# Small q, go, out and dq transfers moved from the POOL queue to the sync queue of an attention backward kernel, with the stores queued early

## The chip, the cores and the metric

The kernel runs on one core of a Trainium2 chip. The metric is device time in microseconds (us) of that core. A ratio is the mean time of one kernel's fast runs over the mean time of the other's fast runs of the same rounds, with a 95% interval; so it is not quite the ratio of the medians that are quoted. "SyncE" (SP in the profile) is the engine that issues the large transfers; "the sync queue" is its hardware DMA queue (q1), "the POOL queue" is the software DMA queue (q0) that POOL issues.

## The reference

Grouped attention with its gradients: 32 batches, 32 query heads, 4 key/value heads, 4 query rows, 2048 keys, head size 128, bfloat16.

```python
B, Hq, Hkv, Sq, Sk, D = 32, 32, 4, 4, 2048, 128
def _fwd_reference(q, k, v):                 # k, v repeated 8 times over the heads
    scores = jnp.einsum("bhqd,bhkd->bhqk", q, k) * D ** -0.5
    p = _softmax(scores, axis=-1)
    return jnp.einsum("bhqk,bhkd->bhqd", p, v)
def reference(q, k, v, grad_out):
    _out, _vjp = jax.vjp(_fwd_reference, q, k, v)
    return (_out, *_vjp(grad_out))           # out, dq, dk, dv
```

Each batch reads 2 MB of K and 2 MB of V and writes 2 MB of dK and 2 MB of dV, in transfers of 1 MB. Beside them are four small transfers of 32 KB a batch: q and go (grad_out) in, out and dq out. In all 274 MB move, of which the small ones are 4.2 MB.

## The kernel before

The program is a list of units (one matmul group, one eviction, one transfer), each with a planned time `PLACE` plus a correction `SHIFT` for the first three and last four batches. The planned times are used only to sort: every engine and every DMA queue then runs its units in that order, waiting where a result is missing.

```python
DMA, SMALL = "SP", "POOL"
PERIOD = 21.3
PLACE = dict(LQ=[-47.936], LK=[...], LV=[3.599, 0.95], ..., Oe=[18.672], Os=[94.455],
    DQe=[52.911], DQs=[136.569], ..., DVs=[39.32, 39.758], DKs=[48.837, 48.854], ...)
# [cut: SHIFT of batches 0, 1, 2 and of the last four, -4 to -1]
u.at = b * PERIOD + PLACE[name][i] + (SHIFT[special][name][i] if special in SHIFT else 0.0)
return sorted(order, key=lambda u: u.at), bank_of

sm_pool = pool("small", 4)                    # q, go, o, dq: four buffers each
if name == "LQ":                              # loads q and go of a batch
    t["q"] = sm_pool.tile([P, D], BF16, name="q_sb")
    nc.gpsimd.dma_start(out=t["q"][:], in_=q_r[b])
    t["go"] = sm_pool.tile([P, D], BF16, name="go_sb")
    nc.gpsimd.dma_start(out=t["go"][:], in_=go_r[b])
elif name in ("LK", "LV"):                    # 1 MB each
    nc.sync.dma_start(out=whole[:, h], in_=src[b, g][:, h])
elif name in ("Os", "DQs"):                   # stores of out and dq; Oe, DQe evict them
    nc.gpsimd.dma_start(out=(o_r if name == "Os" else dq_r)[b], in_=...)
elif name in ("DVs", "DKs"):                  # 1 MB each; the last batch uses halves, DVh and DKh
    nc.sync.dma_start(out=(dv_r if name == "DVs" else dk_r)[b, g], in_=...)
```

## Time and profile before

692.51 us, median of three runs (691.18 to 692.68). The page of the profiled run; the third line is the busy share of the 16 DMA engines in 40 slices, in tenths, and the last is the chain that ended last, by line.

```profile
span 688.6 us, 28403 instructions
...
PE 620.1 (90%) x12352; PEld 467.1 (68%) x12352; DVE 558.3 (81%) x776; ACT 604.4 (88%) x921; POOL 208.8 (30%) x426
...
DMA  9999999999999999999999999999999999999967
GB/s 347 403 413 387 415 414 409 415 415 416 415 416 416 414 416 412 397 407 413 408 409 405 410 412 414 399 398 412 405 412 405 406 401 397 408 403 386 391 260 263
...
q1 hardware_dynamic: 70784, 268.45, 97.6%
q0 software_dynamic: 4096, 4.20, 1.8%
...
DMA v_sb<-in_v_dram 52%; PE psum L372 10%; PE psum L477 6%; ACT dk_sb L483 4%; ACT dv_sb L483 4%; PE psum L431 3%; DMA out_dram<-dv_sb 2%; ACT e_sb L399 2%; PE psum L442 2%; ACT vt_sb L337 2%; POOL dop_sb_103 L411 1%; PE psum L383 1%; DVE kt_sb L390 1%; ACT kt_sb L337 1%; DMA go_sb<-in_grad_out_dram 1%
```

The DMA engines are full in all but the last two slices. Total time is therefore the work of DMA, plus whatever time DMA is made to stand idle, plus the end of the last batch.

The timeline of SyncE (start, us taken, line, what, count) shows it held by queue room, 2.3 to 2.6 us for a 1 MB issue:

```profile
437.64 2.41 SPq L358 DMA_DIRECT2D k_sb<-in_k_dram  x1
440.17 4.67 SPq L492 DMA_DIRECT2D out_dram<-dv_sb  x2
```

The last two slices by windows (window, its us, busy us of PE, PEld, DVE, ACT, POOL, granted clock, DMA share, GB/s), and the whole of SyncE's end:

```profile
654.20:671.40 17.20, 14.27 (x310) 10.23 (x310) 14.47 (x22) 13.97 (x20) 6.80 (x15) 1.00 0.67 260
671.40:688.60 17.20, 8.04 (x200) 5.22 (x196) 8.83 (x9) 6.72 (x10) 1.42 (x3) 0.88 0.73 263
```

```profile
652.89 1.00 SPq L492 DMA_DIRECT2D out_dram<-dv_sb  x2
665.05 0.88 SPq L492 DMA_DIRECT2D out_dram<-dk_sb  x2
669.70 4.89 SPq L488 DMA_DIRECT2D out_dram<-dv_sb  x4
676.83 3.70 SPq L488 DMA_DIRECT2D out_dram<-dk_sb  x4
```

### The profile page before, as it was taken

The numbers are of one execution on the slowest core, as the hardware profiler recorded it, in microseconds if no ns is written. First come the engines' busy times: TensorE is split into PE (matmuls) and PEld (weight loads), VectorE is DVE, ScalarE is ACT, GpSimd is POOL, SyncE is SP. The second block draws the span as 40 slices with busy tenths as digits, with TensorE's granted clock in tenths as the row PEclk, the third lists the DMA queues.
The fourth block names the chain that finished last, engine by engine and source line by source line (L and its number), as shares of the span: only waits on it lengthen the run. The fifth ranks groups of instructions, "written<-read, shape, count | busy, mean of one in ns | idle before, by whom it ended". The sixth has DMA issues, their size and how long they took to land.

```text
span 688.6 us, 28403 instructions
## 1 busy us (share of the span) xinstructions
PE 620.1 (90%) x12352; PEld 467.1 (68%) x12352; DVE 558.3 (81%) x776; ACT 604.4 (88%) x921; POOL 208.8 (30%) x426
## 2 busy tenths in 40 slices
PE   5899999999999999999999899998889998989984
PEld 4677677777677777766667666676666766766753
DVE  3788888888889888888788878787787887888885
ACT  2889999999999999998899888899888998888883
POOL 2423321333322233331233321333212333113330
PEclk9999999999999999999999999999999999999998
DMA  9999999999999999999999999999999999999967
GB/s 347 403 413 387 415 414 409 415 415 416 415 416 416 414 416 412 397 407 413 408 409 405 410 412 414 399 398 412 405 412 405 406 401 397 408 403 386 391 260 263
DMA packets 75005, 274.47 MB, mean 399 GB/s; under 512 B 6272, under 2 KB 6272, under 8 KB 74880
## 3 DMA queue, kind: packets, MB, share of 16 engines
q1 hardware_dynamic: 70784, 268.45, 97.6%
q0 software_dynamic: 4096, 4.20, 1.8%
q8 instruction: 96, 1.57, 0.8%
q14 instruction: 29, 0.24, 0.1%
HBM read 136.31 MB, written 136.31 MB: 396 GB/s over the span
## 4 chain that ended last, share of the span: by engine, by line
DMA 55%; PE 22%; ACT 13%; issue 5%; POOL 3%; DVE 2%; SPq 0%; POOLq 0%; DVEq 0%; ACTq 0%
DMA v_sb<-in_v_dram 52%; PE psum L372 10%; PE psum L477 6%; ACT dk_sb L483 4%; ACT dv_sb L483 4%; PE psum L431 3%; DMA out_dram<-dv_sb 2%; ACT e_sb L399 2%; PE psum L442 2%; ACT vt_sb L337 2%; POOL dop_sb_103 L411 1%; PE psum L383 1%; DVE kt_sb L390 1%; ACT kt_sb L337 1%; DMA go_sb<-in_grad_out_dram 1%
## 5 line engine op out<-in xcount | busy, mean ns | idle before, releaser
L483 ACT CAST dk_sb<-psum 128x1024 bf16<-128x1024 f32 x159 | 157.6, 1013 | 25.9 <-PE psum L477 24.5
L483 ACT CAST dv_sb<-psum 128x1024 bf16<-128x1024 f32 x155 | 151.7, 1022 | 13.2 <-PE psum L477 12.4
L372 PE MATMUL psum<-ident,v_sb 128*128 128x128 bf16 x2048 | 147.4, 220 | 16.8 <-DMA v_sb<-in_v_dram 15.3
L372 PEld LDWEIGHTS <-v_sb 128*128 128x128 bf16 x2048 | 117.9, 98 | 56.9 <-issue 32.8
L372 PE MATMUL psum<-ident,k_sb 128*128 128x128 bf16 x2048 | 142.4, 221 | 10.2 <-ACT dk_sb L483 10.2
L372 PEld LDWEIGHTS <-k_sb 128*128 128x128 bf16 x2048 | 121.4, 99 | 27.1 <-issue 24.3
L483 DVE CAST dv_sb<-psum 128x1024 bf16<-128x1024 f32 x101 | 122.8, 1220 | 10.8 <-PE psum L477 10.6
L483 DVE CAST dk_sb<-psum 128x1024 bf16<-128x1024 f32 x97 | 115.9, 1219 | 8.5 <-ACT kt_sb L337 4.5
L337 ACT COPY kt_sb<-psum 128x512 f32<-128x512 f32 x190 | 110.3, 595 | 6.6 <-PE psum L372 5.1
L411 POOL TENSOR_SCALAR dop_sb_103<-go_sb,rinv 32x128 bf16<-32x128 bf16 x64 | 38.5, 602 | 225.4 <-DVE rinv L404 97.3
L411 POOL TENSOR_SCALAR dop_sb_102<-go_sb,rinv 32x128 bf16<-32x128 bf16 x64 | 38.5, 602 | 212.5 <-DVE rinv L404 141.1
L463 DVE SCALAR_TENSOR_TENSOR ds_sb<-psum,delta,e_sb 128x1024 bf16<-128x1024 f32 x64 | 81.9, 1279 | 15.1 <-ACT vt_sb L337 13.5
L337 ACT COPY vt_sb<-psum 128x512 f32<-128x512 f32 x131 | 75.5, 599 | 17.6 <-PE psum L372 16.6
L340 DVE COPY vt_sb<-psum 128x1024 bf16<-128x1024 bf16 x125 | 82.9, 681 | 2.9 <-PE psum L372 2.6
L477 PEld LDWEIGHTS <-e_sb 64*128 64x128 bf16 x1024 | 50.0, 93 | 36.3 <-issue 19.6
L399 ACT ACTIVATE e_sb<-psum,m 128x1024 bf16<-128x1024 f32 x64 | 71.1, 1122 | 2.4 <-DVE kt_sb L390 2.2
L340 DVE COPY kt_sb<-psum 128x1024 bf16<-128x1024 bf16 x66 | 44.9, 685 | 18.8 <-PE psum L372 18.8
L477 PEld LDWEIGHTS <-ds_sb 64*128 64x128 bf16 x1024 | 43.3, 94 | 23.8 <-issue 8.8
L477 PE MATMUL psum<-dop_sb_103,e_sb 64*128 64x256 bf16 x512 | 45.2, 270 | 4.1 <-POOL dop_sb_103 L411 1.6
L477 PE MATMUL psum<-dop_sb_102,e_sb 64*128 64x256 bf16 x512 | 44.9, 270 | 3.2 <-ACT dv_sb L483 0.7
L390 DVE TENSOR_SCALAR_CACHE_REDUCE kt_sb<-psum 128x1024 bf16<-128x1024 f32 x32 | 39.2, 1225 | 9.6 <-issue 7.7
L390 DVE TENSOR_SCALAR_CACHE_REDUCE kt_sb<-psum,m 128x1024 bf16<-128x1024 f32 x32 | 41.1, 1284 | 6.5 <-DVE kt_sb L390 3.9
(83 smaller groups left out, 764.5 us busy)
## 6 DMA issues: line engine op xcount, KB each, us to landing
k_sb<-in_k_dram SPq DMA_DIRECT2D x62, 1024.0 KB, 18.7
v_sb<-in_v_dram SPq DMA_DIRECT2D x62, 1024.0 KB, 19.6
out_dram<-dv_sb SPq DMA_DIRECT2D x62, 1024.0 KB, 19.0
out_dram<-dk_sb SPq DMA_DIRECT2D x62, 1024.0 KB, 18.8
k_sb<-in_k_dram SPq DMA_DIRECT2D x4, 512.0 KB, 5.4
v_sb<-in_v_dram SPq DMA_DIRECT2D x4, 512.0 KB, 9.4
out_dram<-dv_sb SPq DMA_DIRECT2D x4, 512.0 KB, 7.9
out_dram<-dk_sb SPq DMA_DIRECT2D x4, 512.0 KB, 6.7
```

Source lines behind the costliest of these rows:

```text
L337: nc.scalar.copy(out=out.rearrange("p c d -> p (c d)").bitcast(FP32), in_=in_.rearrange("p c d -> p (c d)").bitcast(FP32))
L340: nc.vector.tensor_copy(out=out, in_=in_)
L372: nc.tensor.transpose(out=ps[:, j, :], in_=t[x, h][:, 8 * i + j, :], identity=ident[:])
L383: nc.tensor.matmul(t[name, i][r, QW * w:QW * w + QW], lhsT=t["qdt"][:, side, r], rhs=t[x, h, i][:, CPQ * w:CPQ * w + CPQ, :], start=True, ...
L390: nc.vector.tensor_scalar(out=spent, in0=t["S", i][:], scalar1=-scale, scalar2=t["m"][:] if i else None, op0=ALU.mult, op1=ALU.min, accum_ ...
L399: nc.scalar.activation(out=t["e"][:, 2 * QW * i:2 * QW * i + 2 * QW], in_=t["S", i][:], func=ACT.Exp, bias=t["m"][:], scale=scale, accum_o ...
L411: nc.gpsimd.tensor_scalar(out=t["dop"][r, h % 2, :], in0=t["go"][r, :], scalar1=t["rinv"][r, :], scalar2=None, op0=ALU.mult)
L431: nc.tensor.transpose(out=ps[:, j, :], in_=src[:, P * c:P * c + P], identity=ident[:])
L442: nc.tensor.matmul(t[name][r, 0:D], lhsT=t[xt, c // 8][:, c % 8, r], rhs=t[x, h][:, c, :], start=(c == 0), stop=(c == C - 1), tile_positio ...
L463: nc.vector.scalar_tensor_tensor(out=t["ds"][:, w], in0=t["DP", i][:], scalar=t["dl"][:], in1=t["e"][:, w], op0=ALU.subtract, op1=ALU.mult)
L477: nc.tensor.matmul(accs[g][:, 2 * P * j:2 * P * j + 2 * P], lhsT=t[lhs][r, P * c:P * c + P], rhs=t[rhs][r, :, :].rearrange("p h d -> p (h ...
L483: copy(out=t[name[:2], "out", g][:, :, CPQ * i:CPQ * i + CPQ, :], in_=t[name[:2], i][g][:].rearrange("p (c h d) -> p h c d", h=2, d=D))
```

## The change

The intent: one hardware queue for all transfers, no software descriptors, and the o and dq buffers freed early. On POOL the stores stood four batches after their results, in pairs. Now they stand 6.3 us (out) and 6.1 us (dq) of the plan after the eviction, and in the first three and last four batches they take the same SHIFT as the eviction. The place of the q and go loads (LQ) is not changed, only their queue.

```diff
-    O=[...], Oe=[18.672], Os=[94.455], DQ=[...], DQe=[52.911],
-    DQs=[136.569], ...
+    O=[...], Oe=[18.672], Os=[25.0], DQ=[...], DQe=[52.911],
+    DQs=[59.0], ...
# [cut: in each of the seven SHIFT tables Os becomes Oe's value and DQs becomes DQe's, e.g.]
-        Oe=[158.875], Os=[319.648], DQe=[601.801], DQs=[743.423],
+        Oe=[158.875], Os=[158.875], DQe=[601.801], DQs=[601.801],
@@ LQ
-            nc.gpsimd.dma_start(out=t["q"][:], in_=q_r[b])
+            nc.sync.dma_start(out=t["q"][:], in_=q_r[b])
-            nc.gpsimd.dma_start(out=t["go"][:], in_=go_r[b])
+            nc.sync.dma_start(out=t["go"][:], in_=go_r[b])
@@ Os, DQs
-            nc.gpsimd.dma_start(out=(o_r if name == "Os" else dq_r)[b], in_=...)
+            nc.sync.dma_start(out=(o_r if name == "Os" else dq_r)[b], in_=...)
```

More of the change, by code (lines that the diff above doesn't have):

```diff
@@ L30 @@
     qp=[18.579], rs=[18.682], ET=[13.658, 17.08], ETe=[14.252, 17.097], DT=[33.736, 36.072], DTe=[35.413, 37.066],
-    O=[17.693, 18.002, 18.156, 18.29], Oe=[18.672], Os=[94.455], DQ=[49.509, 49.546, 51.434, 51.658], DQe=[52.911],
-    DQs=[136.569], DL=[19.54], qfree=[23.411], ofree=[103.245], rfree=[77.997], DP=[19.952, 20.297, 32.139, 32.573],
+    O=[17.693, 18.002, 18.156, 18.29], Oe=[18.672], Os=[25.0], DQ=[49.509, 49.546, 51.434, 51.658], DQe=[52.911],
+    DQs=[59.0], DL=[19.54], qfree=[23.411], ofree=[103.245], rfree=[77.997], DP=[19.952, 20.297, 32.139, 32.573],
     DS=[20.684, 33.191], DV=[17.102, 19.055, 20.709, 23.293], DVe=[18.269, 19.578, 20.009, 20.012, 22.48, 21.535,
@@ L47 @@
         qp=[-26.573], rs=[12.305], ET=[-63.892, -40.448], ETe=[-47.865, -38.526], DT=[-4.086, -0.412], DTe=[-3.298,
-        6.139], O=[-39.845, -33.444, -32.183, -28.165], Oe=[-27.877], Os=[-59.712], DQ=[1.765, 2.888, 1.329, 1.269],
-        DQe=[1.892], DQs=[-81.021], DL=[-24.403], qfree=[-3.591], ofree=[-33.901], rfree=[9.398], DP=[-14.103,
+        6.139], O=[-39.845, -33.444, -32.183, -28.165], Oe=[-27.877], Os=[-27.877], DQ=[1.765, 2.888, 1.329, 1.269],
+        DQe=[1.892], DQs=[1.892], DL=[-24.403], qfree=[-3.591], ofree=[-33.901], rfree=[9.398], DP=[-14.103,
         -13.278, -0.13, 0.179], DS=[-3.43, 2.07], DV=[-22.144, -22.96, -21.745, -14.349], DVe=[-21.142, -24.454,
@@ L60 @@
         0.721], L=[7.117], dop=[8.675], qp=[10.349], rs=[25.4], ET=[1.855, 2.426], ETe=[1.513, 3.358], DT=[13.036,
-        7.483], DTe=[12.538, 6.893], O=[3.459, 3.832, 3.884, 5.102], Oe=[4.915], Os=[-60.332], DQ=[0.889, 1.045,
-        -0.411, 0.94], DQe=[0.233], DQs=[-25.356], DL=[5.409], qfree=[12.194], ofree=[-66.5], rfree=[13.969],
+        7.483], DTe=[12.538, 6.893], O=[3.459, 3.832, 3.884, 5.102], Oe=[4.915], Os=[4.915], DQ=[0.889, 1.045,
+        -0.411, 0.94], DQe=[0.233], DQs=[0.233], DL=[5.409], qfree=[12.194], ofree=[-66.5], rfree=[13.969],
         DP=[6.763, 7.072, 3.675, 3.981], DS=[7.015, 3.749], DV=[6.331, 5.5, 3.952, 3.37], DVe=[5.694, 4.344, 4.713,
@@ L73 @@
         qp=[5.002], rs=[10.293], ET=[1.766, 0.607], ETe=[1.259, 1.305], DT=[0.213, -2.004], DTe=[-0.525, -2.044],
-        O=[1.246, 1.5, 1.545, 1.726], Oe=[1.403], Os=[-52.917], DQ=[1.425, 1.546, 0.484, 0.395], DQe=[-0.47],
-        DQs=[-55.959], DL=[0.669], qfree=[3.492], ofree=[-33.606], rfree=[5.069], DP=[1.794, 1.829, 0.034, -0.258],
+        O=[1.246, 1.5, 1.545, 1.726], Oe=[1.403], Os=[1.403], DQ=[1.425, 1.546, 0.484, 0.395], DQe=[-0.47],
+        DQs=[-0.47], DL=[0.669], qfree=[3.492], ofree=[-33.606], rfree=[5.069], DP=[1.794, 1.829, 0.034, -0.258],
         DS=[2.187, -0.275], DV=[3.733, 2.494, 1.983, 0.34], DVe=[2.697, 1.941, 1.905, 2.434, 1.012, 1.581, 0.049,
@@ L85 @@
         qp=[7.309], rs=[42.149], ET=[2.195, -1.278], ETe=[1.919, -1.171], DT=[4.743, 3.278], DTe=[5.609, 3.25],
-        O=[-1.322, -1.479, 0.528, 1.287], Oe=[1.058], Os=[87.413], DQ=[8.174, 8.908, 7.1, 7.978], DQe=[8.064],
-        DQs=[153.09], DL=[1.413], qfree=[433.476], ofree=[379.582], rfree=[188.9], DP=[2.141, 2.215, 0.855, 0.51],
+        O=[-1.322, -1.479, 0.528, 1.287], Oe=[1.058], Os=[1.058], DQ=[8.174, 8.908, 7.1, 7.978], DQe=[8.064],
+        DQs=[8.064], DL=[1.413], qfree=[433.476], ofree=[379.582], rfree=[188.9], DP=[2.141, 2.215, 0.855, 0.51],
         DS=[2.76, 0.829], DV=[2.494, 0.835, 0.895, 0.758], DVe=[1.61, 0.109, 1.229, 0.024, -0.073, 2.137, -1.76,
@@ L97 @@
         dop=[6.256], qp=[8.124], rs=[52.601], ET=[1.369, 4.066], ETe=[2.632, 4.831], DT=[11.561, 14.267],
-        DTe=[13.249, 14.741], O=[4.22, 3.956, 3.979, 4.659], Oe=[5.161], Os=[124.411], DQ=[53.76, 58.627, 71.647,
-        76.742], DQe=[81.838], DQs=[178.343], DL=[4.74], qfree=[223.784], ofree=[169.959], rfree=[350.347],
+        DTe=[13.249, 14.741], O=[4.22, 3.956, 3.979, 4.659], Oe=[5.161], Os=[5.161], DQ=[53.76, 58.627, 71.647,
+        76.742], DQe=[81.838], DQs=[81.838], DL=[4.74], qfree=[223.784], ofree=[169.959], rfree=[350.347],
         DP=[4.904, 5.645, 9.011, 8.772], DS=[5.688, 11.455], DV=[4.558, 4.643, 5.415, 6.214], DVe=[4.631, 4.282,
@@ L110 @@
         qp=[19.591], rs=[195.2], ET=[16.601, 13.645], ETe=[17.156, 15.506], DT=[91.107, 112.344], DTe=[91.851,
-        123.716], O=[14.871, 15.992, 19.77, 20.459], Oe=[24.605], Os=[65.93], DQ=[226.498, 229.962, 296.861,
-        321.979], DQe=[324.799], DQs=[716.368], DL=[24.893], qfree=[188.487], ofree=[315.264], rfree=[471.673],
+        123.716], O=[14.871, 15.992, 19.77, 20.459], Oe=[24.605], Os=[24.605], DQ=[226.498, 229.962, 296.861,
+        321.979], DQe=[324.799], DQs=[324.799], DL=[24.893], qfree=[188.487], ofree=[315.264], rfree=[471.673],
         DP=[25.295, 26.106, 46.944, 48.701], DS=[28.132, 55.939], DV=[14.792, 16.553, 22.109, 26.604], DVe=[14.274,
@@ L124 @@
         128.051], DT=[266.776, 395.941], DTe=[293.717, 431.921], O=[134.296, 138.938, 140.503, 143.271],
-        Oe=[158.875], Os=[319.648], DQ=[364.485, 371.073, 501.046, 588.268], DQe=[601.801], DQs=[743.423],
+        Oe=[158.875], Os=[158.875], DQ=[364.485, 371.073, 501.046, 588.268], DQe=[601.801], DQs=[601.801],
         DL=[177.07], qfree=[296.09], ofree=[481.606], rfree=[573.081], DP=[203.332, 207.071, 280.92, 280.696],
@@ L452, in emit @@
         elif name in ("Os", "DQs"):
-            nc.gpsimd.dma_start(out=(o_r if name == "Os" else dq_r)[b], in_=t["o" if name == "Os" else "dq"][:])
+            nc.sync.dma_start(out=(o_r if name == "Os" else dq_r)[b], in_=t["o" if name == "Os" else "dq"][:])
         elif name == "DL":
```

## The prediction

> **What bounds the kernel now.** The DMA engines. The page's DMA row is 9 tenths in 38 of 40 slices; the hardware queue takes 97.6% of 16 engines' span, the software queue 1.8% (4.2 of 274 MB). PE is busy 90%, ACT 88%. The chain of waits is V loads back to back from 276 to 616 us, 21.05 us a batch; before that compute sets the pace (20.3 us a batch) while DMA is already full (415 GB/s; later about 405). The timeline of SyncE shows the later stretch limited by queue room: a 1 MB issue takes 2.3 to 2.6 us, against 0.4 us when there is room, and lands 19 us later. The last 34 us (DMA 0.67 and 0.73) are compute and store latency.
>
> **What the change moves.** 128 transfers of 32 KB (4 a batch) leave POOL (0.54 to 0.61 us each, 73 us off an engine that is 30% busy: worth nothing) for SyncE's in-order queue, about 0.4 us an issue. The Trainium skill, "DMA: Bandwidth & Descriptors", section "Issuing engines are not separate DMA queues", says all issuers end on the same 16 engines, so I expect no bandwidth from it; slow 4 KB packets in this trace do not cluster at the software packets either.
>
> **Costs, by term**
> 1. Packets. Software packets here are 2048 B in 84 ns (eight 256 B rows together); hardware packets are one row each (4096 B in 159 ns, 2048 B in 86 ns): about 9 ns plus bytes. Eight 256 B packets would be about 18 ns each (estimate from these), 60 ns more per transfer and engine: 0.24 us a batch, up to +7 us. Taken as +4.
> 2. New head-of-line waits. SyncE must now wait for the dq eviction of batch b before the dv stores of b+1; in the trace those are issued 4.7 to 5.0 us before that eviction in nearly every batch. The o eviction is 5 to 10 us later than the issues now behind it. In steady state the queue holds 10 to 19 us, so these waits only replace waits for room: landings fall to 13 to 16 us, DMA stays full, cost nil. Before 80 us the queue is nearly empty (landings in 6 to 10 us): +3 us.
> 3. A shallower queue may keep the early rate: slow packets (over 200 ns) cost 0.1 to 0.3 us a batch early, about 0.5 to 0.8 late. Taken as -4.
> 4. Tail. The last q/go load (batch 31) is now queued behind the last V loads and lands with them (657 us) instead of before 651; PE is in order, so its transpose holds the last batch's K work: +5. The last dq store stands ahead of one dv and four dk half stores, which now wait for dq's eviction (681.8 us) instead of leaving from 674 to 680: +3.
>
> **Sum:** 692.5 + 4 + 3 - 4 + 8, about 703 us. Range 694 to 714. Faster by over 2%: 0.04; within 2%: 0.62; slower by over 2%: 0.34.
>
> **What the profile would show.** 1: many 256 B packets on the hardware queue, its share up by 2.5 points. 2: SyncE waiting for o and dq evictions; 1 MB issues near 0.4 us after them; landings 13 to 16 us. 3: 410 to 415 GB/s in slices 17 to 36. 4: PE idle for several us near 650 us, released by a q or go load; dk half stores issued after the last dq eviction.
>
> **What would make it wrong.** If 256 B packets are packed (term 1 nil) and the rate recovers, it is the same or slightly faster. If the waits drain the queue in steady state, V loads come late every batch and the loss passes 2%.

## More of the kernel before

The transfers issued between 280 and 550 us, with the median time from issue to landing:

```profile
k_sb<-in_k_dram SPq DMA_DIRECT2D x26, 1024.0 KB, 18.7
...
out_dram<-dv_sb SPq DMA_DIRECT2D x26, 1024.0 KB, 19.3
...
q_sb<-in_q_dram POOLq DMA_DIRECT2D x13, 32.0 KB, 5.8
...
out_dram<-dq_sb POOLq DMA_DIRECT2D x13, 32.0 KB, 6.2
```

A large transfer waits 19 us because seven are under way; a small one on the other queue overtakes them. The Trainium skill ("DMA: Bandwidth & Descriptors", section "Queues, rings and completion order") says that each DMA engine goes round the queues it has work for, a packet at a time; the 5.8 us against 18.7 us agree, without showing the packet as the unit.

The large stores leave as their results come, while the last batches are still being computed.

## The result, and the profile after

719.56 us (718.87 to 720.34, four runs), with before at 692.60 us (691.18 to 694.23, four runs): ratio 1.0393, 95% interval 1.0374 to 1.0411. It is slower by 27 us, outside the predicted range of 694 to 714; the prediction had held "within 2%" (0.62) to be likelier than this (0.34).

```profile
span 718.1 us, 28426 instructions
...
PE 628.1 (87%) x12352; PEld 472.8 (66%) x12352; DVE 558.5 (78%) x776; ACT 603.1 (84%) x921; POOL 132.0 (18%) x298
...
DMA  8999999999999999999999999999999899989539
GB/s 325 363 381 402 344 407 399 413 414 414 413 413 413 409 410 405 404 408 398 410 400 408 409 400 403 407 394 405 396 411 412 324 392 380 377 305 416 225 127 351
```

The middle is close to before. The loss sits in slices 1 to 5 and from slice 32 on: 324, 305, 225 and 127 GB/s, then a flush at 351 when compute is over. The last three slices by windows, in the columns given above:

```profile
664.20:682.20 18.00, 12.93 (x208) 8.92 (x204) 10.40 (x15) 11.32 (x18) 0.00 (x0) 0.81 0.58 228
682.20:700.10 17.90, 15.61 (x348) 11.29 (x340) 17.07 (x23) 13.51 (x20) 4.27 (x10) 1.00 0.34 125
700.10:718.10 18.00, 1.50 (x64) 1.05 (x52) 1.12 (x2) 1.50 (x3) 0.00 (x0) 0.59 0.94 352
```

SyncE's end, to be set against the one of before:

```profile
664.95 0.34 SPq L453 DMA_DIRECT2D out_dram<-o_sb  x1
665.39 0.91 SPq L492 DMA_DIRECT2D out_dram<-dk_sb  x2
682.89 0.34 SPq L453 DMA_DIRECT2D out_dram<-dq_sb  x1
683.33 0.39 SPq L492 DMA_DIRECT2D out_dram<-dv_sb  x1
689.50 0.34 SPq L453 DMA_DIRECT2D out_dram<-o_sb  x1
689.90 1.35 SPq L492 DMA_DIRECT2D out_dram<-dv_sb  x1
698.06 0.34 SPq L453 DMA_DIRECT2D out_dram<-dq_sb  x1
698.45 1.68 SPq L492 DMA_DIRECT2D out_dram<-dk_sb  x2
```

The small store before each group of large ones is issued only when its result exists (682.9, 689.5, 698.1 us), and the large stores behind it stand still until then. By the trace's evictions, the two dv stores of batch 30 were complete at 673.6 us and left at 683.3 and 689.9; its dk stores were complete at 686.2 us and left from 698.5. In the kernel before, the same dv stores left at the moment the eviction ended, 652.9 us. So 6 MB are still to be issued after 698 us.

PE's waits for q (engine, line, for what: us in total, times, longest), in the kernel after:

```profile
PE psum L361 <- DMA q_sb<-in_q_dram: 11.7, 4, 4.7
```

and in the kernel before, where the one wait for q is the start of the program:

```profile
PE psum L361 <- DMA q_sb<-in_q_dram: 6.0, 1, 6.0
```

The timeline of PE puts two new ones at 612 us (4.7 us) and 671 us (4.3 us); the first, with the wait in brackets:

```profile
612.16 0.29 PE L361 MATMUL psum<-ident,q_sb 128*128 128x128 bf16 x1 [4.74 <-DMA q_sb<-in_q_dram]
```

By the order of the sync queue the two are the q loads of batches 29 and 31, issued at 596.8 and 657.3 us; that of batch 30 stands earlier, beside that of batch 28. Each wait also cost more than its length: the trace records a granted TensorE clock of 0.5 from 611.3 to 618.1 us and from 669.3 to 676.1 us, and the matmuls of L372 took 311 to 315 ns there in place of 220. The 0.81 in the window above comes from the second of these. How much of the loss is due to the clock no run separates.

Landings of the large transfers between 280 and 550 us fell to 13 to 16 us:

```profile
v_sb<-in_v_dram SPq DMA_DIRECT2D x26, 1024.0 KB, 13.3
...
out_dram<-dk_sb SPq DMA_DIRECT2D x25, 1024.0 KB, 15.8
out_dram<-dq_sb SPq DMA_DIRECT2D x13, 32.0 KB, 11.1
...
q_sb<-in_q_dram SPq DMA_DIRECT2D x11, 32.0 KB, 14.6
```

I had expected that, but not for this reason. The trace shows that the program uses eight completion semaphores in turn for each queue, so SyncE waits for the transfer eight places back before it issues the next. Before, all eight places of the sync queue were large transfers and the queue itself stopped at seven. Now small ones take places. Counting transfers issued and not yet landed, five or six large ones are under way in most of the stretch, and three, for moments two, where five small ones come in a row (q and go of batches 28 and 30, dq of batch 24):

```profile
555.04 0.62 SPq L347 DMA_DIRECT2D q_sb<-in_q_dram  x1
557.31 1.13 SPq L349 DMA_DIRECT2D go_sb<-in_grad_out_dram  x1
559.86 0.33 SPq L347 DMA_DIRECT2D q_sb<-in_q_dram  x1
560.28 0.62 SPq L349 DMA_DIRECT2D go_sb<-in_grad_out_dram  x1
562.48 0.34 SPq L453 DMA_DIRECT2D out_dram<-dq_sb  x1
565.21 3.08 SPq L492 DMA_DIRECT2D out_dram<-dv_sb  x2
```

The issues are short, but most stand one large landing (2.6 us) apart, and DMA falls to 324 GB/s in that slice.

The packets are as predicted: 16,384 packets of 256 B on the sync queue, mean 18.2 ns, in place of 2048 packets of 2048 B on the POOL queue, mean 87.9 ns (counted in the packets of the traces).

### The profile page after: what moved, and what is told of

Same layout as the page of the kernel before. It is cut to its first block, busy times and chain, and to the rows that moved or that the text cites. A ratio compares the mean times of both kernels' runs of the same rounds, so it can differ in the third digit from the quotient of the medians.

```text
span 718.1 us, 28426 instructions
## 1 busy us (share of the span) xinstructions
PE 628.1 (87%) x12352; PEld 472.8 (66%) x12352; DVE 558.5 (78%) x776; ACT 603.1 (84%) x921; POOL 132.0 (18%) x298
## 4 chain that ended last, share of the span: by engine, by line
DMA 49%; PE 26%; ACT 14%; issue 3%; DVE 3%; SPq 2%; POOL 1%; DVEq 0%; ACTq 0%; POOLq 0%
DMA v_sb<-in_v_dram 17%; DMA out_dram<-dk_sb 14%; DMA k_sb<-in_k_dram 12%; PE psum L372 11%; PE psum L477 7%; DMA q_sb<-in_q_dram 5%; ACT dk_sb L483 4%; PE psum L431 4%; ACT dv_sb L483 4%; ACT e_sb L399 3%; PE psum L442 2%; ACT vt_sb L337 2%; PE psum L383 2%; POOL dop_sb L411 1%; SPq L358 1%
## 5 line engine op out<-in xcount | busy, mean ns | idle before, releaser
L411 POOL TENSOR_SCALAR dop_sb<-go_sb,rinv 32x128 bf16<-32x128 bf16 x128 | 76.4, 597 | 543.7 <-PE psum L431 398.6
L372 PE MATMUL psum<-ident,v_sb 128*128 128x128 bf16 x2048 | 149.4, 222 | 22.1 <-DMA v_sb<-in_v_dram 20.1
L372 PEld LDWEIGHTS <-v_sb 128*128 128x128 bf16 x2048 | 119.6, 98 | 62.5 <-issue 32.1
L372 PE MATMUL psum<-ident,k_sb 128*128 128x128 bf16 x2048 | 144.9, 224 | 14.6 <-ACT dk_sb L483 10.2
L372 PEld LDWEIGHTS <-k_sb 128*128 128x128 bf16 x2048 | 123.3, 100 | 32.1 <-issue 24.4
L477 PE MATMUL psum<-dop_sb,e_sb 64*128 64x256 bf16 x1024 | 90.7, 272 | 7.1 <-POOL dop_sb L411 1.6
L477 PE MATMUL psum<-qp_sb,ds_sb 64*128 64x256 bf16 x1024 | 81.8, 274 | 2.6 <-DVE ds_sb L463 1.3
L419 POOL TENSOR_SCALAR qp_sb<-q_sb,rinv 32x128 bf16<-32x128 bf16 x128 | 46.8, 366 | 10.5
L431 PE MATMUL psum<-ident,ds_sb 128*128 128x128 bf16 x512 | 39.4, 221 | 7.2 <-ACT e_sb L399 7.2
## 6 DMA issues: line engine op xcount, KB each, us to landing
k_sb<-in_k_dram SPq DMA_DIRECT2D x62, 1024.0 KB, 12.9
v_sb<-in_v_dram SPq DMA_DIRECT2D x62, 1024.0 KB, 13.2
```

Of the source, the lines that this page charges most:

```text
L372: nc.tensor.transpose(out=ps[:, j, :], in_=t[x, h][:, 8 * i + j, :], identity=ident[:])
L411: nc.gpsimd.tensor_scalar(out=t["dop"][r, h % 2, :], in0=t["go"][r, :], scalar1=t["rinv"][r, :], scalar2=None, op0=ALU.mult)
L419: nc.gpsimd.tensor_scalar(out=t["qp"][r, h % 2, :], in0=t["q"][r, :], scalar1=t["rinv"][r, :], scalar2=scale, op0=ALU.mult, op1=ALU.mult)
L431: nc.tensor.transpose(out=ps[:, j, :], in_=src[:, P * c:P * c + P], identity=ident[:])
L477: nc.tensor.matmul(accs[g][:, 2 * P * j:2 * P * j + 2 * P], lhsT=t[lhs][r, P * c:P * c + P], rhs=t[rhs][r, :, :].rearrange("p h d -> p (h ...
```

## The experiments

H stands for the theory that SyncE, which works in order, stands in front of small stores whose results are not there; L for late q and go loads stalling PE; P for packets and places in the queue, a cost spread over all batches. Edits are against the kernel before or after, as said.

How far each trace is behind the kernel before, in us, at the end of the dq eviction that is the n-th in time (from 0), and at the end of the span:

| dq eviction | after | e1 | e2 | f2 | f3 | h1 |
|---|---|---|---|---|---|---|
| 4 | 0.9 | -0.3 | 1.4 | 1.1 | 0.5 | -0.5 |
| 12 | 5.1 | 0.0 | 6.0 | 5.8 | 4.2 | 0.6 |
| 25 | 7.8 | 4.5 | 7.8 | 10.2 | 7.8 | 3.5 |
| 27 | 17.4 | 12.7 | 7.9 | 10.9 | 8.5 | 4.1 |
| 31 | 21.0 | 15.4 | 7.6 | 10.0 | 7.1 | 3.0 |
| end | 29.6 | 15.5 | 15.5 | 18.2 | 7.5 | 3.1 |

The loss of the kernel after has three parts: 7.8 us by the 25th, 13.2 us from there to the last, and 8.6 us after the last dq eviction.

### e1, e2, e3, e4: one part of the change at a time

e1 moves only the loads (before, with the two LQ lines on `nc.sync`). e2 moves only the stores (after, with the two LQ lines back on `nc.gpsimd`). e3 keeps all on POOL and changes only the places:

```diff
# e3, against after
-            nc.sync.dma_start(out=t["q"][:], in_=q_r[b])        # and go, and Os/DQs
+            nc.gpsimd.dma_start(out=t["q"][:], in_=q_r[b])
```

e4 moves all four to the sync queue at the old places (before, with `nc.sync` in all three lines).

> Only the q and go loads move to the sync queue; stores stay on POOL at their old places. Theory H (the loss is SyncE waiting in order for o and dq results, worst in the last five batches): little of the 27 us, about +8 us: packets +3, the last two q loads +5 in place of +9 because the rest of the queue is not stalled. Theory L (late q and go loads stall PE at the end): most of the loss, +18 or more, with PE waiting some 9 us for q_sb. Theory P (packets and queue room everywhere): about half, +13, spread evenly over the batches.

> Only the o and dq stores move to the sync queue, at their new early places; loads stay on POOL. H: most of the loss, +16 to +20 us, with SyncE waiting over 10 us for dq near the end and DMA idle between 670 and 700 us. L: small, +5. P: about +13, even over the batches.

> All small transfers stay on POOL; only the order changes, o and dq stores soon after their results. H: within 3 us of before, because big transfers cannot be held by them; POOL may hold dop a little, +0 to +4. If the early places themselves were the harm (POOL waiting for o or dq ahead of dop), +8 or more. L and P: same as before.

> All small transfers go to the sync queue, at the old late places of the stores, so their results are ready when SyncE gets there. H: no waits for o or dq, so about +12 us: packets +6, last q loads +5. L: nearly the whole loss, over +20. P: nearly the whole loss, over +20, even over the batches.

Measured, with before at 692.62 us (691.39 to 693.43):

| run | us | ratio (95%) |
|---|---|---|
| e1, loads only | 706.70 (703.65 to 708.00) | 1.0202 (1.0172 to 1.0232) |
| e2, stores only | 705.90 (705.19 to 707.18) | 1.0199 (1.0181 to 1.0217) |
| e3, places only | 692.93 (692.32 to 694.25) | 1.0014 (0.9993 to 1.0035) |
| e4, queue only | 711.45 (710.76 to 713.48) | 1.0282 (1.0261 to 1.0303) |

Loads (+14) and stores (+13) add up to the whole. I had put the loads at +8: a miss. The loads lose mostly at the end, from the 25th dq eviction on (column e1). The stores lose by the 12th and again after the last (column e2). e3 settles that early places alone do no harm: POOL waits there for dq and o too, but no large transfer stands behind it.

e4 shows why the change had to bring the stores forward. ACT's waits:

```profile
ACT dq_sb L449 <- DMA out_dram<-dq_sb: 21.7, 10, 9.5
```

A store queued four batches late lands another 11 us later on this queue, and the four dq buffers are then all taken. So e4 brought a new wait and is not a clean test of H.

### f1: e4 with five o and dq buffers

```diff
# against e4
+    od_pool = pool("od", 5)
-            t[x] = sm_pool.tile([P, D], BF16, name=x + "_sb")
+            t[x] = od_pool.tile([P, D], BF16, name=x + "_sb")
```

> As e4 (all small transfers on the sync queue, stores at their old late places), but o and dq have 5 buffers each in place of 4. In e4 ACT waited 21.7 us in 10 times for an old dq store to land before it could write the next dq. If that was e4's own cost, those waits go and the batch-7 jump of 9 us is gone. What is left is then loads (+15.4 in e1) plus what the stores cost without any wait for unready results: about +16 to +19 in all, and the after kernel's +27 minus this is what the early places cost. If the early places cost nothing, this kernel is as slow as after, +27.

710.05 us (709.23 to 712.63) against 694.20 (691.89 to 696.24): 1.0242 (1.0205 to 1.0280). The waits for a dq buffer are gone and the mid-run lag fell (12.5 us behind at the 25th dq eviction in place of e4's 22.3), yet the end is about the same. The two lags do not add: in e4 the earlier stall had hidden the late q loads, and in f1 PE's waits for q are back. SyncE in f1 also waits before 55 us for the first o and dq, because in the first batches the old places are not late; by the dq of batch 4 it had moved 50.5 MB, less than after (51.4). It agrees in size with its expectation, but does not separate H from P.

### f2: q and go loads of the last four batches at their normal distance

```diff
# against after
+for _b in (-4, -3, -2, -1):
+    SHIFT[_b]["LQ"] = [0.0]
```

The edit takes away the corrections of these loads. By the plan those of batches 28, 29 and 31 come 17, 36 and 53 us earlier, and that of batch 30, which had stood beside batch 28's, comes 21 us later.

> The after kernel with the q and go loads of the last four batches at their normal distance (earlier in the queue). Theory L for the tail: PE no longer waits for q_sb near 600 and 660 us, 9 to 11 us faster than after, about 709 us. If the last V loads set the tail anyway, at most 3 us faster.

707.42 us (706.89 to 708.60): 1.0200 (1.0167 to 1.0233) against the same before of 694.20. That is 12 us faster than after. PE's waits in f2 (its L364 is L361 of the kernels above, three lines down):

```profile
PE psum L364 <- DMA q_sb<-in_q_dram: 4.5, 2, 2.7
```

Both lie before 15 us of the span, so the two near the end are gone. The lag no longer grows after the 25th dq eviction (10.2 there, 10.0 at the last). What remains is the lag gained by then and the 8 us after it. The edit also parts the two neighbouring q and go pairs, so it does not say how much of the 12 us was PE waiting and how much was places taken by small transfers. The lags give a hint: in the kernel after, 3.1 us came between the 25th dq eviction and the next (604.6 us), before PE's first long wait for q, and 10.1 us after that.

### f3: in addition, the last small stores behind all large stores

```diff
# against f2
+for _b in (-3, -2, -1):
+    SHIFT[_b]["Os"] = SHIFT[_b]["DQs"] = [1500.0]
```

> As f2, and the o and dq stores of the last three batches stand behind every large store, so that no large store waits for a dq or o that is not there yet. Theory H for the end: 7 to 9 us faster than f2, about 701 us, DMA not idle between the last V load and the end. If the end is set by compute alone: the same as f2.

699.67 us (697.85 to 701.28): 1.0094 (1.0055 to 1.0133) against 694.20, another 8 us faster. After the last dq eviction f2 falls 8.2 us behind, f3 0.4 us. The last windows of f3:

```profile
660.00:680.00 20.00, 17.52 (x384) 12.75 (x380) 17.59 (x26) 16.69 (x25) 4.44 (x10) 1.00 0.89 352
680.00:696.10 16.10, 6.58 (x163) 4.14 (x152) 7.37 (x8) 5.79 (x9) 0.00 (x0) 0.90 0.68 242
```

The slice at 0.34 is gone. H is shown for the end.

### f4: is the depth of the queue worth something?

```diff
# against before: each 1 MB transfer as two of 512 KB, same 4096 B packets
-            for h in range(2) if b == 0 else [slice(0, 2)]:
+            for h in range(2):
# [cut: the same loop over h around the store of DVs and DKs]
```

> The kernel before, small transfers on POOL as they were, but each 1 MB load and store cut in two 512 KB ones with the same 4096 B packets. The program waits for the transfer 8 places back before it issues the next, so at most 4 MB are under way in place of 7; landings fall from 19 to about 10 us. Theory D (a shorter queue costs, because the deep one lets stores lag and hides them under the last batches): +5 to +10 us, gained between batches 5 and 14, constant after. If depth is free as I predicted: within 2 us of before.

701.03 us (700.61 to 703.00) against 694.20: 1.0112 (1.0077 to 1.0146). Neither theory holds as written. There is a loss in the span of 10 us, but none of it by the 12th dq eviction (-0.2 us); it grows slowly after that. ACT has a wait of another kind:

```profile
ACT dk_sb L483 <- DMA out_dram<-dv_sb: 17.7, 13, 2.1
```

It waits for dv stores to free an output buffer, which it does for 0.5 us in the kernel before. So halving the transfers disturbs more than depth, and what depth alone is worth is not settled by this run. h1 below answers part of it.

### g1: the first three batches' small stores later

```diff
# against f3
+for _b in (0, 1, 2):
+    SHIFT[_b]["Os"] = [SHIFT[_b]["Os"][0] + 25.0]
+    SHIFT[_b]["DQs"] = [SHIFT[_b]["DQs"][0] + 20.0]
```

> As f3, and the o and dq stores of the first three batches stand 20 to 25 us later in the queue. In the after kernel SyncE waits 7.8, 9.9, 8.6 and 6.1 us for o or dq before 85 us, and by the dq of batch 4 DMA has moved 51.4 MB where the kernel before has moved 54.1 at the same time; at 0.41 MB a us that is 6.5 us of work. Theory H (these waits are the lost work): 54 MB by batch 4, no jump of 5 us between batches 8 and 14, and 3 to 5 us faster than f3, about 696 us. Theory P (smaller packets and fewer transfers under way cost the 7 us): the same as f3, about 699 us.

697.29 us (696.61 to 697.78) against 692.67 (690.58 to 696.19): 1.0057 (1.0015 to 1.0098). No proof: 51.8 MB were moved by the dq of batch 4, as in f3. The trace says why: SyncE no longer waited before 75 us, but then for 8.9 us, until 84.0 us, for the o of batch 3, which I had not moved. The edit only shifted the wait, so h1 was made.

### h1: every small store one batch later

```diff
# against f3
+PLACE["Os"], PLACE["DQs"] = [46.3], [80.3]      # 25.0 + 21.3, 59.0 + 21.3
```

> As f3, but every o and dq store stands exactly one batch (21.3 us of the plan) later in the same place of the sync queue's order, so its result is always there when SyncE comes to it, at the start as well, and the buffers are still free in time. g1 had only moved the waits of the start to the o of batch 3. Theory H: SyncE no longer waits for o or dq anywhere, 54 MB moved by the dq of batch 4, and 3 to 5 us faster than f3, about 696 us; what is left over before (3 to 4 us) is packets. Theory P (packets and fewer transfers under way): the same as f3, 1.009 times before, with 52 MB at batch 4.

693.50 us (693.10 to 696.45, six runs) against 693.33 (691.60 to 695.88, eleven runs): 1.0016 (0.9992 to 1.0040): the same as before, with all transfers on the sync queue. The first 85 us as one window, in the order before, after, f3, h1, each from its own trace:

```profile
0.00:85.00 85.00, 71.04 (x1330) 54.24 (x1331) 61.82 (x90) 66.13 (x104) 27.94 (x63) 1.00 1.00 393
```

```profile
0.00:85.00 85.00, 71.97 (x1322) 54.93 (x1322) 61.29 (x90) 65.26 (x103) 18.31 (x46) 1.00 0.97 360
```

```profile
0.00:85.00 85.00, 71.18 (x1333) 54.00 (x1335) 62.12 (x91) 66.41 (x104) 18.26 (x46) 1.00 0.98 369
```

```profile
0.00:85.00 85.00, 71.67 (x1335) 54.24 (x1337) 62.29 (x91) 66.41 (x104) 18.31 (x46) 1.00 1.00 391
```

The last column is the rate. The kernel after moves 33 GB/s less for 85 us, 2.8 MB; h1 has nearly all of it back. By the dq of batch 4 it had moved 53.7 MB (before 54.1, f3 51.8). SyncE's longest waits for a small store's result before 90 us, in after and then in h1 (whose store line is L459):

```profile
SPq L453 <- ACT o_sb L449: 21.6, 3, 9.8
SPq L453 <- DVE dq_sb L451: 7.7, 1, 7.7
```

```profile
SPq L459 <- ACT o_sb L455: 0.9, 1, 0.9
```

H is shown for the start too. The edit moved these stores in every batch; that the gain is one of the start is read from the table, where f3 is 4.2 us behind at the 12th dq eviction and h1 0.6, and f3 gains no more on h1 after that (7.1 and 3.0 at the last). P is not shown: h1 has the same small packets and lets the same small transfers take places (V loads land in 13.3 us as in after), and it costs at most 0.4% by its interval. In its trace it is 3.1 us behind; that is the room left for packets and places together.

### g2, g3

g2 takes the batches from memory in the opposite order. g3 puts the last two V loads ahead of two dv stores (`SHIFT[-1]["LV"] = [-7.0, -4.3]`), both against before.

> The kernel before with the batches taken from memory in the opposite order; outputs stay correct. Nothing else changes. In before and after alike, slow 4096 B packets (over 200 ns) grow from 0.1 to 0.5 us a batch at about 270 us. If that follows memory addresses, the slow stretch now comes first and the fast one late. If it follows time or the state of the queue, it starts near 270 us again. My prediction had tied it to the depth of the queue, which the after kernel already speaks against.

> The kernel before with the last two V loads issued ahead of the two dv stores of batch 29. If the last V landing sets the end, up to 5 us faster; as PE waited only 1.1 us for it, 0 to 2 us faster is my guess. An attempt at a version that beats both.

g2 took 691.54 us in its single run, whose state is unknown. The time that 4096 B packets took beyond 159 ns, summed over the packets and divided by the 16 engines, was 0.4 us between 215 and 258 us and 1.3 us in the next 43 us. In the kernel before it goes from 0.4 to 1.1 us in the same stretches. So the slow packets do not follow the address. They do not become fewer with a shallower queue either: the kernel after, with 13 us landings, goes from 0.5 to 1.1 us there. In e1, e4, f1, f2, f3 and g1 they had already grown between 215 and 258 us (0.9 to 1.5 us), in f4 and h1 between 172 and 215 us. The cause is open. g3 took 694.38 us (693.80 to 697.57): 1.0025 (0.9984 to 1.0066), no gain. No version beat both kernels.

## Why the prediction was wrong

The direction and the mechanisms were named; the sum was 16 us short (703 against 719.6). By its own terms:

- **Term 4, the tail, +8, is the step that failed by its size.** Undoing it in two edits gave back 12 us (f2) and 8 us (f3). "The last q/go load (batch 31)" did land with the last V loads and stalled PE for 4.3 us, about the +5 given to it; but it was one of three trouble spots: the load of batch 29 stalled PE as long (4.7 us), and five small transfers in a row near 560 us emptied the queue. "The last dq store stands ahead of one dv and four dk half stores" named the one store that cost nothing to speak of: it was issued at 704.0 us, 1.2 us after its eviction and in step with the issues around it. I had listed the order of the whole tail but costed only its last entry: the dq of batch 29, the out of batch 31 and the dq of batch 30 held 4 MB of dv and dk, 10 to 16 us after they were ready.
- **Term 3, -4, was wrong.** Slow packets did not become fewer at 13 us landings; in the kernel after they came with the same onset as before, in h1 earlier. The predicted 410 to 415 GB/s in slices 17 to 36 did not come: most were between 394 and 412.
- **Term 2 was right in kind, and too small at the start.** "+3" measured about 4 us in the traces (the lag at the 25th dq eviction is 7.8 us in f3 and 3.5 us in h1) and 5 to 6 between the runs. It appears late: until about the eighth batch compute sets the pace, so 2.8 MB not moved early show as time only when DMA becomes the limit. "DMA stays full, cost nil" in the middle held, and so did landings of 13 to 16 us; but the cause of the shorter landings was mostly the eight semaphores in turn, which I had not seen: h1, where SyncE hardly waits for results, has landings of 13 to 16 us too.
- **Term 1, +4, was right in the packet and a little high in the cost.** 18 ns a packet was measured as 18.2. Eight of them in place of one packet of 88 ns is 57.7 ns on each DMA engine for each of 128 transfers, 7.4 us of packet time. In h1's trace 3.1 us of lag is left for it and for everything else, and 0.4% of the time is 2.8 us.
- The statement that leaving the POOL queue gains nothing held: h1 is within 0.4% of before. It agrees with the Trainium skill, "DMA: Bandwidth & Descriptors", section "Issuing engines are not separate DMA queues", which says that transfers started by any engine run on the same 16 DMA engines.

Of the 27 us, about 12 are thus the loads of the last four batches, 8 the stores of the last three, and 6 the remaining waits for o and dq, most of them at the start: the steps from 719.6 to 707.4, 699.7 and 693.5 us. The runs are from different rounds, in which before varied by up to 1.6 us in its median; by the ratios to before, each of its own rounds, the steps are 13, 7 and 5 us, and the 1 us that is left is within the noise.

## What to carry to other kernels

A queue that is issued in order turns a small store with a missing result into a wait for everything behind it. Place such a store where its result is surely there: one batch later in the same order, and behind the large stores in the last three batches, took back the whole cost of the early places. When a load joins a full queue, plan it earlier by at least what its landing grew (here from 5.8 to 14.6 us; the exact distance was not tested), and look first at the beginning and the end of the program, where the order was tuned for another queue. Cost every entry of the new order there, not the last one alone.

## What the Trainium skill lacked or had wrong

- "DMA: Bandwidth & Descriptors", section "Issuing engine by pattern", recommends the sync queue for simple loads and stores. Here small ones on POOL were as fast for the kernel and landed sooner: they landed in 5.8 us beside a full sync queue and in 11 to 15 us on it, and POOL's waits held no large transfer (e3: 1.0014).
- The same page, "Why small descriptors are slow (HBM only)", gives 11 cycles for a 256 B descriptor on the bus inside a DMA engine. At the page's 850 MHz that is 12.9 ns (an estimate from the page); the trace has 18.2 ns a packet of 256 B on the hardware queue, which may count more than the bus. The page "DMA: Bandwidth & Descriptors" does not say that the software queue joined eight such rows into one packet of 84 to 88 ns where the hardware queue did not, though its section "SWDGE vs HWDGE vs iDMA" says that a packet may have up to 64 descriptors.
- No page gives the room of the sync queue in transfers. Here an issue blocked at seven transfers of 1 MB under way (17 packets on each engine for one, with the completion packet), and a program with eight completion semaphores in turn let small transfers displace large ones.
- No page says what makes some 4096 B packets take 200 to over 1000 ns in place of 159. They grew near 260 us in the kernel before, in either order of the batches, and in after, and between 172 and 258 us in eight other kernels.
